# Eighteen small loads ahead of the setup of a decode block, and a clearing of where they land

## The chip, the cores and the metric

The kernel runs on one core of a Trainium2 chip. The metric is the device time of one execution in microseconds (us); it was 242.41 us, the median of two runs (242.36 and 242.45). The engines of the core are PE (TensorE, matmuls), DVE (VectorE), ACT (ScalarE), POOL (GpSimd) and SP (SyncE). Each runs its own list of instructions in order and meets the others only at semaphores. Transfers between the chip's memory (HBM) and the core's on-chip memory (SBUF) are issued by an engine into a DMA queue of its own and are carried by 16 DMA engines. PSUM is the memory that matmuls write.

## The reference

One decode step of a transformer block for four sequences, with modulation by a condition `c`:

```
mod = (silu(c) @ w_mod) -> sa, ca, ga, sb, cb, gb
h   = layernorm(x) * (1 + ca) + sa
q   = h @ wq                                  # 32 heads of 128
p   = softmax(q k^T / sqrt(128))              # 8 KV heads, the last 2048 positions
x   = x + ga * ((p v) @ wo)
h   = layernorm(x) * (1 + cb) + sb
x   = x + gb * ((silu(h @ w1) * (h @ w3)) @ w2)
```

All is float32. What has to be read is about 101 MB: `w_mod`, `wq`, seven KV groups of 8.39 MB each with K and V together, the eighth in two parts, `wo`, `w1`, `w3` and `w2`.

## The kernel before

The weights and the KV cache pass through `ring`, a buffer in SBUF of three slots of 64 KB in each of the 128 partitions. The loads go to the slots in turn: `w_mod_a` (the first third of `w_mod`, with `x` and `c` behind it) to slot 0, `wq` to slot 1, KV group 0 (`kv[0]`) to slot 2, then KV group 1 to slot 0 when `w_mod_a` has been used, KV group 2 to slot 1 when `wq` has been used, group 3 to slot 2 when attention of group 0 is done, and so on to the end. SP issues them all but `wq`, which ACT issues (line 186); each issue waits on SP until its slot is free. A KV group is 128 rows of 64 KB, `w_mod_a` 128 rows of 16.5 KB.

Ahead of the attention stands a setup that needs little data. POOL clears and builds `ident` (the identity for transposes), clears `sc`, `hidT`, `qT` and `xs` (lines 193 to 205), and copies `x` from `w_mod_a` into `xs` (line 273). DVE derives `same`, `avg`, `spread` and `pick` from `ident`. ACT computes `e`, the exponential in silu(c) (line 231). Then come the first layernorm, the modulation out of `w_mod_a` (`mod_a`), `hT`, and with it the issue of KV group 1; then `q` out of `wq`, its transposed form `qT`, the issue of KV group 2, and the groups. A group computes scores on PE into `s_ps`, their maximum on DVE (`nm`), the exponential on ACT into `p_sb`, its transposes, the products with V on PE, and a reduction.

The class `Program` records every operation in the order in which the code is written; the profile gives all of them line 57. For every operand it takes a box: the partitions from the first to the last, and the columns from the lowest to the highest that are touched. An operation waits for an earlier one on another engine, and for an earlier DMA on whatever engine, if their boxes overlap and one of the two writes. A DMA has a semaphore of its own that it raises when it has landed; the wait for it stands in the list of the engine that needs it, ahead of the instruction, so everything behind it on that engine waits too. Before the change, `p_sb`, 128 x 2048, is first written by the exponential of group 0.

Of the kernel before, what the change touches and what calls it, by code (L numbers as in the profile page):

```python
# [11 lines left out]
NT = 4  # L12
# [133 lines left out]
def block_kernel(nc, w_mod_a, wq, kv_in, wo_mod, last_k_wo, last_v, wo, w1, w3, w2, out):  # L146
# [5 lines left out]
    do = Program(nc)  # L152

    def sb(name, *shape):
        return nc.alloc_sbuf_tensor(name, (P, *shape), F32).ap()
# [12 lines left out]
    def bank():  # L168
        turn[0] += 1
        return banks[turn[0] % 2]  # L170

    def load(dst, src, cuts=(0, 1), queue="sync"):
        step = src.shape[1] // cuts[-1]
        for lo, hi in zip(cuts[:-1], cuts[1:]):
            do(queue, "dma_start", dst[:, lo * step : hi * step], src[:, lo * step : hi * step])
        return dst[:, : src.shape[1]]

    def batch(t):

        return t[:, ::8]  # L180
# [6 lines left out]
    do("scalar", "preload_act_table_set", "natural_log_exp_and_others")  # L187
    kv = [None] * G
    kv[0] = load(slots[2], kv_in[0])

# [78 lines left out]


    do("gpsimd", "tensor_copy", batch(xs), xt_sb)
    xp = bank()[:, :P]
    do("tensor", "transpose", xp, xs, ident)
    tot = sb("tot", 1)
# [14 lines left out]
    for half in range(2):  # L291
        qp = s_ps[half]
        for k in range(4):
            for i in range(4):
                at = ((half * 4 + i) * 4 + k) * 512
# [18 lines left out]
            do("tensor", "matmul", a_ps[32 * i : 32 * i + B, :], oT[:, g, i, :], wo_t[g][:, i, :], start=(g == 0), stop=(g == G - 1))  # L314

    mx, nm, ls, l, rl = (sb(n, m) for n, m in (("mx", NT), ("nm", 1), ("ls", NT), ("l", 1), ("rl", 1)))
    p_all = sb("p_sb", NT * 512)
    p_sb = [p_all[:, t * 512 : (t + 1) * 512] for t in range(NT)]
    pT = [sb(f"pT{t}", B, NC, R) for t in range(NT)]
    o_own, o_sum = sb("o_own", NC, P), sb("o_sum", P)  # L320
# [194 lines left out]
```

## Time and profile before

| what | value |
|---|---|
| time, median of two runs | 242.41 us |
| profiled execution, span from the first to the last instruction | 241.1 us |
| the rest of a time, outside the span (242.41 - 241.1) | 1.3 us |
| read from HBM | 101.20 MB, 420 GB/s over the span |
| DMA engines busy | 89.5% by SP's queue, 8.1% by ACT's |
| PE busy | 146.8 us (61%) |
| DVE, ACT, POOL busy | 55.2, 24.0, 2.6 us |

The profile of one execution gives for each instruction its start and length in us from the start of the span, and what ended the idle time before it. A "q" behind an engine's name (SPq, ACTq) is its issuing of DMAs. The DMA rows count packets; q1 is the queue of SP and q10 that of ACT. The packets of q10 are 144: the 128 rows of `wq` and 16 more of nearly no bytes, one on each DMA engine, that close the load and raise its semaphore. The chain of waits follows the work that ended last from its end to the start.

### The profile page before, as it was taken

How to read it: one execution, taken by the hardware profiler on the slowest of the kernel's cores; microseconds unless marked ns; L12 is line 12 of the kernel's file. 1: busy time of each engine (PE TensorE's matmuls, PEld its weight loads, DVE VectorE, ACT ScalarE, POOL GpSimd, SP SyncE). 2: the span in 40 equal slices, each digit the busy share in tenths (PEclk: the TensorE clock that was granted, in tenths of full speed). 3: DMA queues.
4: the chain of work that ended last, by engine and by line, in shares of the span. 5: the costliest groups of instructions: out<-in, count | busy, mean ns of one | idle time of the engine just before them, and what ended most of it. 6: DMA issues, size and time to landing. Idle time of an engine off the chain costs nothing.

```text
span 241.1 us, 2468 instructions
## 1 busy us (share of the span) xinstructions
PE 146.8 (61%) x1103; PEld 52.8 (22%) x1103; DVE 55.2 (23%) x140; ACT 24.0 (10%) x36; POOL 2.6 (1%) x11
## 2 busy tenths in 40 slices
PE   0000169756782972945767586567296919964876
PEld 0000132213222312201311222221131202422333
DVE  4000220240303124123132124130312014103120
ACT  2000000103003003001200300300300000320100
POOL 3000000000000000000000000000000000000000
PEclk9999997995977799779797589797977997996899
DMA  8999989898989898989999999999999999999993
GB/s 316 414 436 425 500 370 500 351 511 359 511 359 503 370 502 370 489 383 478 391 479 391 478 394 468 402 468 405 457 413 424 435 405 435 407 432 426 416 415 133
DMA packets 2889, 101.38 MB, mean 421 GB/s; under 512 B 448, under 2 KB 448, under 8 KB 704
## 3 DMA queue, kind: packets, MB, share of 16 engines
q1 hardware_dynamic: 2736, 92.85, 89.5%
q10 hardware_dynamic: 144, 8.39, 8.1%
q8 instruction: 8, 0.13, 0.2%
q14 instruction: 1, 0.01, 0.0%
HBM read 101.20 MB, written 0.03 MB: 420 GB/s over the span
## 4 chain that ended last, share of the span: by engine, by line
DMA 73%; PE 20%; DVE 3%; ACT 2%; issue 0%; SPq 0%
DMA ring<-kv_in 30%; DMA ring<-wo_mod 17%; DMA ring<-w 15%; DMA ring<-w_mod_a 11%; PE s_ps L57 8%; PE bank L57 7%; PE o_ps L57 4%; PE a_ps L57 2%; ACT p_sb L57 2%; DVE nm L57 2%; DVE p_sb L57 0%; DVE e L57 0%; DVE sq L57 0%; DVE xc L57 0%; DVE tot L57 0%
## 5 line engine op out<-in xcount | busy, mean ns | idle before, releaser
L57 PE MATMUL s_ps<-ring,qT 128*32 128x512 f32 x256 | 37.0, 731 | 20.2 <-DMA ring<-kv_in 14.7
L57 PE MATMUL bank<-ident,p_sb 128*128 128x128 f32 (+1 forms) x136 | 27.4, 350 | 30.8 <-ACT p_sb L57 30.7
L57 PE MATMUL o_ps<-ring,pT 128*16 128x512 f32 x256 | 37.8, 696 | 0.0
L57 PEld LDWEIGHTS bank<-ident,p_sb 128*128 128x128 f32 (+1 forms) x136 | 19.6, 177 | 51.9 <-ACT p_sb L57 31.7
L57 ACT ACTIVATE p_sb<-s_ps,nm 128x2048 f32<-128x2048 f32 (+1 forms) x11 | 16.5, 1501 | 143.2 <-DVE oT L57 105.2
L57 DVE TENSOR_REDUCE nm<-s_ps 128x1 f32<-128x2048 f32 x7 | 16.0, 2292 | 34.5 <-PE s_ps L57 34.5
L57 DVE COPY pT<-bank 128x64 f32<-128x64 f32 x32 | 7.2, 224 | 56.1 <-PE bank L57 56.1
L57 PEld LDWEIGHTS s_ps<-ring,qT 128*32 128x32 f32 x256 | 9.0, 131 | 47.5 <-issue 20.7
L57 PE MATMUL bank<-ident,xs 128*128 128x128 f32 x1 | 0.5, 473 | 27.8 <-POOL xs L57 27.8
L57 PE MATMUL s_ps<-ring,h2T 128*32 128x512 f32 (+1 forms) x64 | 9.1, 664 | 2.3 <-DMA ring<-w 2.3
L57 PE MATMUL a_ps<-ring,oT 128*4 128x512 f32 x64 | 9.1, 709 | 2.0 <-DMA ring<-wo_mod 2.0
L57 PE MATMUL s_ps<-ring,hT 128*32 128x512 f32 x64 | 8.8, 711 | 0.4 <-DVE hT L57 0.4
L57 PEld LDWEIGHTS o_ps<-ring,pT 128*16 128x16 f32 x256 | 5.4, 98 | 11.6 <-issue 9.2
L57 DVE SCALAR_TENSOR_TENSOR o_own<-o_ps,rl,own 128x512 f32<-128x512 f32 x7 | 5.3, 751 | 11.1 <-PE o_ps L57 11.1
L57 DVE TENSOR_REDUCE o_sum<-o_own 128x128 f32<-128x512 f32 x7 | 7.2, 1029 | 0.2
L57 PE MATMUL bank<-ring,sc 128*32 128x256 f32 (+1 forms) x64 | 7.2, 610 | 0.0
L57 PEld LDWEIGHTS bank<-ident,xs 128*128 128x128 f32 x1 | 0.2, 180 | 27.8 <-POOL xs L57 27.8
L57 DVE TENSOR_SCALAR e<-e 128x16 f32<-128x16 f32 x1 | 0.2, 174 | 23.8 <-ACT e L57 23.8
L57 DVE TENSOR_REDUCE mx<-s_ps 128x1 f32<-128x512 f32 x4 | 2.8, 691 | 7.6 <-PE s_ps L57 7.6
L57 DVE COPY qT<-bank 128x64 f32<-128x64 f32 x8 | 2.2, 277 | 9.8 <-PE bank L57 9.4
L57 PEld LDWEIGHTS s_ps<-ring,h2T 128*32 128x32 f32 x64 | 2.6, 129 | 7.4 <-issue 4.5
L57 PE MATMUL s_ps<-ring,hidT 128*32 128x64 f32 (+1 forms) x126 | 3.7, 262 | 0.3 <-DVE hidT L57 0.3
(93 smaller groups left out, 55.4 us busy)
## 6 DMA issues: line engine op xcount, KB each, us to landing
ring<-w SPq DMA_DIRECT2D x2, 3584.0 KB, 38.3
ring<-last_k_wo SPq DMA_DIRECT2D x1, 6144.0 KB, 30.5
ring<-last_v SPq DMA_DIRECT2D x1, 4096.0 KB, 39.9
ring<-w_mod_a SPq DMA_DIRECT2D x1, 2064.0 KB, 26.6
ring<-wo SPq DMA_DIRECT2D x1, 2048.0 KB, 43.4
ring<-w SPq DMA_DIRECT2D x1, 1792.0 KB, 40.9
ring<-w SPq DMA_DIRECT2D x1, 1024.0 KB, 42.9
ring<-w SPq DMA_DIRECT2D x1, 512.0 KB, 43.7
```

What stands on the lines that cost most here:

```text
L57: op = Op(engine, lambda: getattr(getattr(self.nc, engine), method)(*args, **kw), [])
```

## The change

Fifteen loads are put into ACT's list behind `wq` and the table load, and three into POOL's list ahead of its setup. All copy a piece of `w1` that no computation uses into the first 819 columns of `p_sb`, whose allocation moves up for it. After its last piece of setup, POOL clears the first 1024 columns of `p_sb`.

```diff
     do("scalar", "preload_act_table_set", "natural_log_exp_and_others")
     kv = [None] * G
     kv[0] = load(slots[2], kv_in[0])
+    p_all = sb("p_sb", NT * 512)
+    marks = p_all[:, :1024]
+    for n in range(1, 16):
+        do("scalar", "dma_start", marks[:n, 32 * n : 32 * n + 4 * n], w1[:n, 32 * n : 32 * n + 4 * n])
+    for n in range(3):
+        at, m = 512 + 128 * n, 17 + n
+        do("gpsimd", "dma_start", marks[:8, at : at + 64].rearrange("p (s c) -> p s c", s=2)[:, :, :m], w1[:8, at : at + 64].rearrange("p (s c) -> p s c", s=2)[:, :, :m])
...
     do("gpsimd", "tensor_copy", batch(xs), xt_sb)
+    do("gpsimd", "memset", marks, 0.0)
     xp = bank()[:, :P]
...
-    p_all = sb("p_sb", NT * 512)
```

Load n of ACT has n rows of 4n floats and lies at columns 32n to 36n. From n = 9 on its last columns reach into those of load n + 1 (load 9 ends at 324, load 10 begins at 320), and load 15 ends at 540, behind the beginning of POOL's first at 512. The lists show what `Program` makes of that.

ACT's list at the start of the program, before the change (a number in brackets is a semaphore; part0_22_0 is that of `w_mod_a`):

```order
L57 DMA ring<-wq 128x16384 [waits barrier_Pool_Activation_PE_DVE_SP_release]
L57 ACT_TABLE_LOAD
L57 ACTIVATE e<-ring 128x16 [waits part0_22_0]
L57 ACTIVATE ln<-bank,eps_t 128x1 [waits part0_22_tensor,part0_22_vector]
L57 ACTIVATE r<-ln 128x1 [waits part0_22_scalar]
```

And the same place now, from load 7 on; part0_40_12 to part0_40_17 are the semaphores of loads 9 to 14, and part0_40_0 is again that of `w_mod_a`:

```order
L57 DMA p_sb<-w 7x28
L57 DMA p_sb<-w 8x32
L57 DMA p_sb<-w 9x36
L57 DMA p_sb<-w 10x40 [waits part0_40_12]
L57 DMA p_sb<-w 11x44 [waits part0_40_13]
L57 DMA p_sb<-w 12x48 [waits part0_40_14]
L57 DMA p_sb<-w 13x52 [waits part0_40_15]
L57 DMA p_sb<-w 14x56 [waits part0_40_16]
L57 DMA p_sb<-w 15x60 [waits part0_40_17]
L57 ACTIVATE e<-ring 128x16 [waits part0_40_0]
```

Loads 1 to 9 have no wait; each of the loads 10 to 15 stands behind a wait for the landing of the one before it, and `e` now stands behind them all.

POOL's list from the start barrier to its last work, before:

```order
L57 MEMSET ident 128x132 [waits barrier_Pool_Activation_PE_DVE_SP_gather]
L57 ISA [waits part0_22_gpsimd]
L57 AFFINE_SELECT ident<-ident 128x128
L57 MEMSET sc 128x128
L57 MEMSET hidT 128x504
L57 MEMSET qT 128x1024
L57 MEMSET xs 128x128
L57 COPY xs<-ring 128x16 [waits part0_22_0,part0_22_gpsimd]
```

And now; part0_40_18 is the semaphore of ACT's load 15, and those of the last row are of loads that nothing ahead has waited for:

```order
L57 DMA p_sb<-w 8x2x17 [waits barrier_Pool_Activation_PE_DVE_SP_gather,part0_40_18]
L57 DMA p_sb<-w 8x2x18
L57 DMA p_sb<-w 8x2x19
L57 MEMSET ident 128x132
L57 ISA [waits part0_40_gpsimd]
L57 AFFINE_SELECT ident<-ident 128x128
L57 MEMSET sc 128x128
L57 MEMSET hidT 128x504
L57 MEMSET qT 128x1024
L57 MEMSET xs 128x128
L57 COPY xs<-ring 128x16 [waits part0_40_0,part0_40_gpsimd]
L57 MEMSET p_sb 128x1024 [waits part0_40_5,part0_40_6,part0_40_4,part0_40_7,part0_40_21,part0_40_8,part0_40_20,part0_40_9,part0_40_19,part0_40_10,part0_40_11]
```

The wait for load 15 stands at the head of the list, ahead of all of POOL's setup, and the exponential of group 0 on ACT waits for the clearing of `p_sb`. The lists of PE, DVE and SP are the same as before.

## The prediction

> **What bounds the kernel now.** First the page: span, busy share of the DMA engines, and the chain of waits by engine.
>
> ```profile
> span 241.1 us, 2468 instructions
> DMA  8999989898989898989999999999999999999993
> ...
> DMA 73%; PE 20%; DVE 3%; ACT 2%; issue 0%; SPq 0%
> ```
>
> The DMA engines are busy in every slice but the last, and three quarters of the chain is waiting for data. The table of stretches says the same by stage (the last two columns are DMA share and GB/s).
>
> ```profile
> 34.50:47.30 12.80, 10.05 (x72) 3.24 (x73) 2.69 (x11) 1.19 (x2) 0.00 (x0) 0.87 0.95 411
> 47.30:67.30 20.00, 12.34 (x86) 4.58 (x84) 6.34 (x13) 2.06 (x2) 0.00 (x0) 0.83 0.97 419
> 67.30:85.50 18.20, 13.91 (x82) 4.91 (x82) 3.33 (x7) 2.06 (x2) 0.00 (x0) 0.72 1.05 455
> 183.60:229.80 46.20, 33.46 (x239) 11.13 (x239) 9.35 (x32) 5.32 (x14) 0.00 (x0) 0.85 0.98 421
> ```
>
> There is no hole in the stream from which lost time could be won back later. So an edit costs what it holds up the stream of loads, and nothing otherwise. The stream holds as long as the next load is issued before the last one ends. Next, then, the issues of KV groups and the waits for them.
>
> ```profile
> 34.46 0.33 SPq L57 DMA_DIRECT2D ring<-kv_in  x1
> 64.81 59.09 SPq L57 DMA_DIRECT2D ring<-kv_in  x4
> ...
> ring<-kv_in SPq DMA_DIRECT2D x1, 46.9
> ...
> 48.17 1.07 PE L57 MATMUL s_ps<-ring,qT 128*32 128x512 f32 x8 [0.57 <-DMA ring<-kv_in]
> 67.28 5.34 PE L57 MATMUL s_ps<-ring,qT 128*32 128x512 f32 x32 [2.54 <-DMA ring<-kv_in]
> 86.77 3.64 PE L57 MATMUL s_ps<-ring,qT 128*32 128x512 f32 x32 [1.32 <-DMA ring<-kv_in]
> ```
>
> Group 0 is issued at 1.15 (the SP row below) and lands 46.9 us later, at 48.05. Group 1 is issued at 34.46, 13.6 us ahead of that, lands at 67.28, and group 2 at 86.77. In the stream a group takes 19.5 us.
>
> **The change, part by part.** It removes nothing; it adds 18 tiny loads, one clearing and, as the lists show, waits. What decides is when ACT's load 9 lands, since loads 10 to 15, `e`, and all of POOL's setup follow it one by one.
>
> **When load 9 lands.** The issues at the start, and the DMA packets up to 14 us, up to 26 us and from 26 to 27.5 us:
>
> ```profile
> 0.73 0.39 ACTq L57 DMA_DIRECT2D ring<-wq  x1
> 0.74 0.36 SPq L57 DMA_DIRECT2D ring<-w_mod_a  x1
> 1.15 33.64 SPq L57 DMA_DIRECT2D ring<-kv_in  x2
> ...
> q10 hardware_dynamic: 64, 4.19, 70.9%
> q1 hardware_dynamic: 64, 1.06, 20.2%
> ...
> q10 hardware_dynamic: 128, 8.39, 75.4%
> q1 hardware_dynamic: 128, 2.11, 20.3%
> ...
> q1 hardware_dynamic: 32, 1.05, 161.8%
> q10 hardware_dynamic: 16, 0.00, 0.6%
> ```
>
> Two things are read here. Up to 26 us both queues have sent the same number of packets, 64 and 64, then 128 and 128, though a row of `wq` is four times one of `w_mod_a`: a DMA engine takes one packet from one queue, then one from the other. And no row of `kv_in` has gone before `w_mod_a` ends, though it was issued at 1.15: a queue is served in order. In 26 to 27.5 us come the 16 closing packets of `wq`, those of `w_mod_a`, and the first 16 rows of group 0.
>
> So ACT's small loads, issued by about 7 us (9 times the 0.39 us of `wq`'s issue), stay behind `wq` till about 27 us. From then on the two queues take turns again: each small packet goes between two 64 KB rows of group 0, of which each DMA engine has 8 (128 rows by 16). A small load costs an engine that carries it a row and a closing packet; load 9 is the ninth, so the engine that carries all nine has 18 packets to send and 8 turns for them. Even if each load cost but one packet there, nine are more than eight. Load 9 therefore lands with the end of group 0 or just behind, **at 48.3 us** (48.05 and, for what is left of the tiny packets, some 0.3 by my estimate).
>
> The Trainium skill speaks against this: its page "DMA: Bandwidth & Descriptors", section "Queues, rings and completion order", says that an engine takes turns by packets of typically 9 to 17 descriptors. By that, load 9 would be out after one turn; the equal counts above are against it, and its result is the first rival below.
>
> **Loads 10 to 15.** Each waits for the landing of the one before it, now with no other transfer under way. The nearest row is the only small transfer of the trace, the output (KB, us from issue to landing), and how soon ACT starts once its data is there is seen at `e`:
>
> ```profile
> out<-p_sb SPq DMA_DIRECT2D x1, 32.0 KB, 1.5
> ...
> 0.74 26.62 DMA ring<-w_mod_a
> 27.38 0.22 ACT L57 ACTIVATE e<-ring 128x16 f32<-128x16 f32 x1 [24.94 <-DMA ring<-w_mod_a]
> ```
>
> `w_mod_a` lands at 27.36, `e` starts at 27.38. I take 1.6 us for a step, the 1.5 of the output and a little for the wait; six make 9.6, and load 15 lands **at 57.9**. The ends: 1.5 (9.0 in all), since issue and landing can't be shorter than for a transfer that met no other either, and 2.2 (13.2), if reading HBM costs half as much again. The Trainium skill, same page, section "Anatomy of one DMA — SWDGE (gpsimd) path", gives about 2.0 us of fixed cost for a DMA of GpSimd's; six of these would end 2.4 us later than by my value.
>
> **POOL's three loads.** The trace before has no DMA issued by POOL. Bounds per load: the 0.33 us of SP's issue from below, a whole step of 1.6 and as much again for building it from above (3.2). I take 0.9, nearer to the row of an issue, and 2.7 for three, so that `ident` is begun **at 60.6** (ends: 58.9 and 67.5).
>
> **From there to the issue of group 1.** POOL's setup and what DVE makes of it used to lie beside the load of `w_mod_a`, and cost nothing. That cover is gone:
>
> ```profile
> 0.73 0.21 POOL L57 MEMSET ident<- 128x132 f32 x1 [0.29 <-POOLq L508]
> 1.18 0.29 POOL L57 TENSOR_SCALAR_AFFINE_SELECT ident<-ident 128x128 f32<-128x128 f32 x1 [0.23 <-POOL ident L57]
> 2.90 0.20 POOL L57 MEMSET xs<- 128x128 f32 x1
> 27.50 0.21 POOL L57 COPY xs<-ring 128x16 f32<-128x16 f32 x1 [24.39 <-DMA ring<-w_mod_a]
> ...
> 27.76 0.47 PE L57 MATMUL bank<-ident,xs 128*128 128x128 f32 x1 [27.76 <-POOL xs L57]
> ...
> 1.96 0.37 DVE L57 TENSOR_REDUCE same<-ident 128x32 f32<-128x128 f32 x1
> 3.54 0.25 DVE L57 TENSOR_REDUCE pick<-pick_c 128x16 f32<-128x64 f32 x1
> 27.63 0.17 DVE L57 TENSOR_SCALAR e<-e 128x16 f32<-128x16 f32 x1 [23.84 <-ACT e L57]
> 28.27 0.29 DVE L57 COPY x_sb<-bank 128x128 f32<-128x128 f32 x1
> ```
>
> `ident` is begun at 0.73 and ready at 1.47, 0.75 later. DVE's work on it runs from 1.96 to 3.79, 1.83; `e` through DVE from 27.63 to the copy of `x_sb` at 28.27, another 0.64. Together 3.2 us from `ident` to `x_sb`. POOL's own way is no longer: 2.37 us to the end of clearing `xs` (0.73 to 3.10), 0.21 for the copy, 0.5 for PE's transpose (27.76 to 28.27 lies behind the copy), 3.1. From `x_sb` to the issue of group 1 it is 28.27 to 34.46, 6.2. So 9.5 us in all with the steps between engines, and group 1 is issued **at 70.1** instead of 34.46.
>
> **What that does to the stream.** Group 0 has landed at 48.05 and nothing else has been issued: the DMA engines stand still. A load issued into an empty queue takes its 19.5 us and what an issue needs to get going, at most the 1.5 us of the output's whole way; I take 21.2, and group 1 lands at 91.3 instead of 67.28, **24.0 us later**.
>
> Does the delay stay? The issues of groups 2 and 4, and PE's wait for the last K:
>
> ```profile
> 45.73 40.12 SPq L57 DMA_DIRECT2D ring<-kv_in  x3
> ...
> 85.52 39.92 DMA ring<-kv_in
> ...
> 198.26 5.16 PE L57 MATMUL s_ps<-ring,qT 128*32 128x512 f32 x32 [5.45 <-DMA ring<-last_k_wo]
> ```
>
> From group 1's issue, group 2's came 11.3 us later, group 3's 30.4 (64.81). Measured from the new issue, the stream would run dry at 40.7 (two groups, 21.2 + 19.5), so group 3's comes 10 us ahead. Group 0 now ends after group 1 has landed, so attention lags the loads by some 9 us (30.4 less 21.2); but a group's compute is 18.2 us (67.28 to 85.52, when the slot of group 1 was free and group 4 was issued) and its load 19.5, so the lag shrinks by over 1 us in each of the six groups that follow, and the 5.5 us for which PE waited for the last K take the rest. The stream runs on, 24.0 us late, to its end. Clearing `p_sb` (128x1024, as `qT`, whose clearing lies within POOL's 2.37 us above) is done some 4 us after `ident` is begun, 15 us before the exponential of group 0, and costs nothing. Bytes are no matter: 18 loads of less than 4 KB.
>
> The sum is made against the profiled execution: 241.1 + 24.0 = 265.1 us of span, and with the 1.3 us outside it 266.4; I say **266 us**. A difference within 2% of the time, 4.8 us, is about what a measurement of this kernel can tell from no change.
>
> **The rivals.**
> *The small packets don't take turns one by one.* If the first nine loads pass in one turn, load 9 lands at about 29 us, behind one row of group 0 (19.5 / 8 = 2.4 us from 27). Each of loads 10 to 15 then waits for one row (2.4 us, six: load 15 at 44) or for two, one ahead of its data and one ahead of its closing packet (4.9 us, four till 48.6, then two of 1.6: at 52). With 12.2 us to the issue and 21.2 to landing, group 1 lands at 77 to 85, 10 to 18 us late: 252 to 260, middle 257. For it speaks only that no packet as small as these stands among large ones in the trace; against it the equal counts.
> *The handshakes are dear.* Steps at 2.2 and POOL's loads at 2.5 each add 3.6 and 4.8: 275 us. No row excludes it.
> *Not slower.* If the small loads went ahead of the rest of `wq`, load 9 would be there at some 8 us (issues till 7, and the 1.5 of a landing), and six steps of 3.0 (a row of each queue, 19.5 / 8 and a quarter of it) bring load 15 to 26. All is then hidden as long as group 1 is issued by about 46.5, 1.5 ahead of the end of group 0; with 9.5 and 2.7 behind load 15, that is up to a load 15 at 34.3. The price is nothing: 242 us. Against it stands the order within q1, where group 0 stood still behind `w_mod_a` for 25 us.
>
> **How the numbers follow.** My forecast has 0.66, with a range of its own of 262 to 271 (steps from 1.5 to 2.0, POOL's loads from 0.33 to 1.9 each). The first rival has 0.13, the dear handshakes 0.16, not slower 0.04, and 0.01 is for a start that is faster for some other reason. The range reaches into the first rival's upper half and takes in the dear handshakes: **256 to 276**. Slower by over 2% are all but the last two: 0.95; within 2% 0.04; faster 0.01.
>
> **What would show it.** The packets of ACT's queue spread over 27 to 48 us between those of SP's; ACT idle till past 57 us and six issues some 1.6 us apart from 48 us on; `ident` begun at about 60 us; DMA slices near zero from 48 to 71 us and full behind; group 1's issue at 70; the same tail, 24 us later. It is wrong if load 9 lands well before 48, if POOL's loads take more than 2 us each, or if attention of the first groups, started late, becomes the limit behind the hole.

## The result, and the profile after

The changed kernel takes 266.14 us (two runs, 265.97 and 266.31) against 242.41: a ratio of 1.098, 95% interval 1.096 to 1.100. The forecast was 266.0, slower.

The page of the changed kernel: span, the busy tenths of DVE and POOL, the DMA engines' by slices of 6.6 us, and the chain by engine.

```profile
span 264.6 us, 2492 instructions
...
DVE  1000000005205133152241231231332011313031
...
POOL 0000000043000000000000000000000000000000
...
DMA  9999997000897999999899989998999899999994
...
DMA 47%; PE 37%; DVE 7%; ACT 5%; issue 1%; ACTq 1%; POOL 1%; POOLq 0%; DVEq 0%
```

The span is 23.5 us longer than the 241.1 before. Where there was no hole in the DMA row there is now one of three empty slices and parts of the two beside them, and POOL's setup, once in the first slice, lies at its end. The stretch around the hole, with the DMA engines' share and GB/s in its last two columns:

```profile
47.60:69.00 21.40, 4.79 (x37) 2.54 (x37) 5.12 (x26) 0.68 (x3) 5.27 (x11) 1.00 0.13 41
```

The chain of waits in order of time (start, length, what) runs through the hole:

```profile
4.26 43.30 DMA p_sb<-w
47.56 0.02 issue
47.58 1.54 DMA p_sb<-w
...
49.15 1.35 DMA p_sb<-w
...
50.52 1.39 DMA p_sb<-w
...
51.94 1.37 DMA p_sb<-w
...
53.33 1.50 DMA p_sb<-w
...
54.85 1.44 DMA p_sb<-w
56.29 0.29 issue
56.58 1.81 POOL p_sb L57 x3
58.39 0.23 POOL ident L57
```

Load 9, issued at about 4 us, lands at 47.56. Each of the six loads behind it is issued when the one before has landed, and takes 1.35 to 1.54 us; load 15 is there at 56.29. POOL builds its three loads in 1.81 us, and only then begins `ident`. Here are the issue of group 1 on SP, and its time to landing (the view leaves out the KB; the number is us):

```profile
67.70 0.33 SPq L57 DMA_DIRECT2D ring<-kv_in  x1
...
ring<-kv_in SPq DMA_DIRECT2D x1, 23.2
```

Group 1 lands at 90.9 us instead of 67.28, 23.6 us later, and the end comes 23.5 us later.

What kept load 9 for 43 us is read from the packets of the two queues, in stretches of about the time of one 64 KB row (2.42 us). The stretches shown are 28.2 to 30.6, 30.6 to 33.0, 33.0 to 35.4, 37.9 to 40.3, 42.7 to 45.1, and last 45.1 to 47.6.

```profile
q1 hardware_dynamic: 16, 1.05, 100.8%
q10 hardware_dynamic: 9, 0.00, 0.3%
...
q10 hardware_dynamic: 9, 0.00, 0.2%
...
q10 hardware_dynamic: 8, 0.00, 0.2%
...
q10 hardware_dynamic: 7, 0.00, 0.2%
...
q10 hardware_dynamic: 6, 0.00, 0.2%
...
q10 hardware_dynamic: 36, 0.00, 1.0%
q1 hardware_dynamic: 16, 0.00, 0.4%
```

In each stretch but the last SP's queue sends 16 rows, one on each engine (its line is shown once, the others are alike but for the share), and ACT's queue a single small packet on those engines that still have some: first the 9 data rows of the nine engines concerned, then 9 closing packets, then 8 for the eight engines that carry a second load, and so on. The other 36 go together at 45.1 to 47.6, when SP's queue has nothing left but the 16 closing packets of group 0. The nine loads have 90 small packets in all, 45 rows and 45 closings: a load of n rows runs on n engines. That is what the Trainium skill states in "DMA: Bandwidth & Descriptors", section "Why a DMA increments its semaphore by 16 and not by 1". The turns of typically 9 to 17 descriptors that the Trainium skill states on the same page (section "Queues, rings and completion order") are not seen here: a turn is one row or one closing packet.

### The profile page after: what moved, and what is told of

Same layout as the page of the kernel before. It is cut to its first block, busy times and chain, and to the rows that moved or that the text cites. A ratio compares the mean times of both kernels' runs of the same rounds, so it can differ in the third digit from the quotient of the medians.

```text
span 264.6 us, 2492 instructions
## 1 busy us (share of the span) xinstructions
PE 146.2 (55%) x1103; PEld 52.6 (20%) x1103; DVE 55.8 (21%) x140; ACT 24.1 (9%) x36; POOL 5.5 (2%) x15
## 4 chain that ended last, share of the span: by engine, by line
DMA 47%; PE 37%; DVE 7%; ACT 5%; issue 1%; ACTq 1%; POOL 1%; POOLq 0%; DVEq 0%
DMA p_sb<-w 20%; PE s_ps L57 17%; DMA ring<-kv_in 16%; DMA ring<-last_k_wo 12%; PE bank L57 10%; PE o_ps L57 9%; ACT p_sb L57 4%; DVE nm L57 4%; ACTq L57 1%; ACT work L57 1%; PE a_ps L57 1%; POOL p_sb L57 1%; DVE avg L57 0%; DVE sq L57 0%; DVE h L57 0%
## 5 line engine op out<-in xcount | busy, mean ns | idle before, releaser
L57 PE MATMUL bank<-ident,p_sb 128*128 128x128 f32 (+1 forms) x136 | 28.1, 356 | 30.8 <-ACT p_sb L57 30.7
L57 PE MATMUL s_ps<-ring,qT 128*32 128x512 f32 x256 | 35.2, 700 | 11.0 <-DMA ring<-kv_in 5.5
L57 PE MATMUL o_ps<-ring,pT 128*16 128x512 f32 x256 | 38.7, 712 | 0.0
L57 ACT ACTIVATE p_sb<-s_ps,nm 128x2048 f32<-128x2048 f32 (+1 forms) x11 | 16.5, 1501 | 134.7 <-DVE oT L57 94.6
L57 PE MATMUL s_ps<-ring,h2T 128*32 128x512 f32 (+1 forms) x64 | 10.0, 715 | 0.4 <-DVE h2T L57 0.4
L57 DVE COPY oT<-bank 128x16 f32<-128x16 f32 x8 | 1.3, 167 | 12.1 <-PE bank L57 12.1
```

What stands on the lines that cost most here:

```text
L57: op = Op(engine, lambda: getattr(getattr(self.nc, engine), method)(*args, **kw), [])
```

## The experiments

All are variants of the changed kernel, each compared with the kernel before on the same chip.

**Without overlaps between the loads** (e1). POOL's boxes and the cleared columns move along.

```diff
-    marks = p_all[:, :1024]
+    marks = p_all[:, :1152]
     for n in range(1, 16):
-        do("scalar", "dma_start", marks[:n, 32 * n : 32 * n + 4 * n], w1[:n, 32 * n : 32 * n + 4 * n])
+        at = 60 * (n - 1)
+        do("scalar", "dma_start", marks[:n, at : at + 4 * n], w1[:n, at : at + 4 * n])
     for n in range(3):
-        at, m = 512 + 128 * n, 17 + n
+        at, m = 900 + 64 * n, 17 + n
...
```

> All 18 loads and the clearing are kept, but no two loads overlap: ACT's loads lie one behind the other from column 0 to 900, POOL's from 900 on, and POOL clears 1152 columns. So no load waits for another; only the clearing waits for all. Theory (the chain of waits makes a hole in the stream of loads, and the hole is the whole loss): the small loads still go one by one between the rows of group 0 and land at about 47.6 us, but e starts at 27.4 us, group 1 is issued at about 34.5 us and the time is that of before, 242.4 us, within 1 us. First rival (the loads themselves cost, by their packets between the large rows or by POOL building them): most of the 24 us stays, some 260 us or more. Second rival (the clearing of p_sb is late for the exponential of group 0, which starts at 54.3 us in the trace before): the clearing begins at 47.6 us and is done by 49 us, so it too gives 242.4 us here; were the time between, the start of that exponential would show it.

Measured: 257.24 us, ratio 1.062 (1.060 to 1.064; here and below the 95% interval stands in brackets). None of the three forecasts held: 14.8 of some 24 us stay, which is most of them but short of the first rival's 260. The lines are two of POOL's (its loads and the clearing), then the exponential of group 0, the issue of group 3, and the DMA share of the stretch between (last two columns: share, GB/s):

```profile
1.35 1.81 POOL L57 DMA_DIRECT2D p_sb<-w  x3 [0.91 <-POOLq L516]
...
86.31 1.06 POOL L57 MEMSET p_sb<- 128x1152 f32 x1 [58.41 <-DMA p_sb<-w]
...
87.49 1.97 ACT L57 ACTIVATE p_sb<-s_ps,nm 128x2048 f32<-128x2048 f32 x1 [40.35 <-POOL p_sb L57]
...
97.14 0.33 SPq L57 DMA_DIRECT2D ring<-kv_in  x1
...
86.00:98.00 12.00, 8.40 (x60) 3.57 (x64) 1.79 (x7) 2.06 (x2) 1.06 (x1) 0.72 0.00 0
```

The start is undisturbed (`e` at 27.57), so group 1 and group 2 are issued in time (34.72 and 45.98), and just that keeps the small loads waiting: the busiest engine now has 30 small packets, and they find 24 rows to stand behind, those of groups 0 to 2. They are through when the stream runs dry at about 86 us; the clearing, the exponential of group 0 and the issue of group 3 follow, and the hole of 12 us lies there. So the clearing was late for the exponential of group 0, as the second rival has it, but at 86 us; what failed is my figure of 47.6, which took the end of group 0 from the changed kernel, where nothing stands behind it. That the loads cost by themselves is not excluded by this run; e8, below, excludes it.

**Eight loads without overlaps** (e9), and **all eighteen into a tile that is needed late** (e8). e9 is e1 with `range(8, 16)`. e8 has the loads without overlaps in `mod_b` (allocated ahead for it), and clears that:

```diff
-    marks = p_all[:, :1024]
+    mod_b = sb("mod_b", 512)
+    marks = mod_b
     for n in range(1, 16):
+        at = 2 * n * (n - 1)
-        do("scalar", "dma_start", marks[:n, 32 * n : 32 * n + 4 * n], w1[:n, 32 * n : 32 * n + 4 * n])
+        do("scalar", "dma_start", marks[:n, at : at + 4 * n], w1[:n, at : at + 4 * n])
     for n in range(3):
-        at, m = 512 + 128 * n, 17 + n
+        at, m = 128 * n, 17 + n
...
```

with POOL's loads in partitions 64 to 71, where they overlap none of ACT's.

> e1_apart with ACT's loads 8 to 15 alone, into p_sb, POOL's three loads and the clearing kept. Theory: 16 packets on the busiest engine, 16 rows of 2.42 us from 27 us on, so the clearing begins at about 66.5 us and the exponential of group 0 at about 67.7 us, 13.4 us later than in the profile before (54.26). Its end frees the slot for group 3 at about 78 us instead of 64.8, still 7 us ahead of the end of the stream's group 2. So nothing is lost: 242.4 us, up to 243. Rival (a loss in proportion to the loads, eight fifteenths of e1_apart's 14.8 us): 250 us.

> All 18 loads, without overlap as in e1_apart, but into mod_b, a tile that the kernel does not use before about 190 us, and POOL clears mod_b (512 columns) in place of p_sb. Nothing early waits for the loads or for the clearing. Theory, mended after e1_apart (a small load has two packets on an engine, each waits for one 64 KB row of the other queue, and the loads go on waiting as long as the stream is kept full): the engine that carries all fifteen has 30 packets, 30 rows of 2.42 us from 27 us on, so the loads are through and the clearing begins at about 100 us; in e1_apart, where the stream ran dry, it was 86.3 us. Time 242.4 us, within 0.7 us. Rival (the loads cost by themselves, in packets or in POOL's building of them): e1_apart's 257 us or part of it.

Measured: e9 242.95 us, ratio 1.002 (1.001 to 1.003); e8 242.67 us, ratio 1.001 (1.000 to 1.002). The clearings, e9's and e8's, and e9's exponential of group 0:

```profile
64.05 1.06 POOL L57 MEMSET p_sb<- 128x1152 f32 x1 [36.21 <-DMA p_sb<-w]
...
65.22 1.97 ACT L57 ACTIVATE p_sb<-s_ps,nm 128x2048 f32<-128x2048 f32 x1 [18.45 <-POOL p_sb L57]
...
93.20 0.53 POOL L57 MEMSET mod_b<- 128x512 f32 x1 [65.36 <-DMA mod_b<-w]
```

In e8 the loads travel for over 60 us and the time is that of before within 0.2 us: the packets themselves, and POOL's building of its loads, cost next to nothing, and with that e1's first rival is excluded. In e9 the exponential of group 0 is 11 us late and group 3 is issued at 75.3 instead of 64.8, with the stream still full: 0.5 us. Both clearings came earlier than expected, by 2.4 and 6.8 us, one row and three. The closing packets of the groups themselves take turns too (one group had closed by then in e9, three in e8: from 28 to 92 us SP's queue sent 464 packets, 26 rows and three closings on each engine). So 16 small packets meet 15 rows and 30 meet 27: 27 us and 15 or 27 times 2.42 are 63.3 and 92.3, and a little under 1 us to landing.

**Which wait holds the start: POOL's loads behind its setup** (e2), **`e` ahead of loads 10 to 15** (e5), **and both** (e6). e2 moves the three lines of POOL's loads behind `do("gpsimd", "tensor_copy", batch(xs), xt_sb)`; e5 splits ACT's loop:

```diff
-    for n in range(1, 16):
+    for n in range(1, 10):
         do("scalar", "dma_start", marks[:n, 32 * n : 32 * n + 4 * n], w1[:n, 32 * n : 32 * n + 4 * n])
+    e = sb("e", 16)
+    do("scalar", "activation", e, ct_sb, AF.Exp, scale=-1.0)
+    for n in range(10, 16):
+        do("scalar", "dma_start", marks[:n, 32 * n : 32 * n + 4 * n], w1[:n, 32 * n : 32 * n + 4 * n])
...
-    e = sb("e", 16)
-    do("scalar", "activation", e, ct_sb, AF.Exp, scale=-1.0)
```

> POOL's three loads stand behind its setup and the copy into xs, right ahead of the clearing; ACT's list is that of the change. Theory: ident is begun at 0.7 us again, but e still stands behind load 15 and starts at 55.2 us as in the profile of the change. From e to the issue of group 1 it is 7.1 us in the trace before (27.38 to 34.46), so the issue comes at 62.3 us instead of 67.7, and the time is 5.4 us below that of the change: 260.7 us. Rival (POOL's position at the head is the whole cause): the setup is free again, group 1 is issued at about 34.5 us, 242.4 us.

> On ACT, e stands behind load 9 and ahead of loads 10 to 15; POOL's list is that of the change, with its loads at the head. Theory: e runs at 27.4 us, but loads 10 to 15 still wait for load 9 at 47.6 us, load 15 lands at 56.3 us, POOL begins ident at 58.4 us, and DVE needs ident before it comes to e. Group 1 is issued at 67.7 us, the time is that of the change, 266 us, within 1 us. Rival (ACT's late e is the whole cause): group 1 at about 34.5 us and 242.4 us.

> Both: e ahead of loads 10 to 15 on ACT, and POOL's loads behind its setup. Theory: neither e nor ident is late, but the next work of ACT, the logarithm of the first layernorm (ln), stands behind load 15 and starts at about 55.3 us; in the trace before it starts at 30.93 us, 3.5 us ahead of the issue of group 1, so the issue comes at 58.8 us, 8.9 us ahead of the change's, and the time is about 257 us. Rival (the late e and the late ident are the whole cause): 242.4 us.

Measured: e2 260.52 us, ratio 1.075 (1.073 to 1.077), `e` at 55.60 and the issue of group 1 at 62.69; e5 266.23 us, 1.098 (1.096 to 1.100), issue at 68.09. So POOL's place sets the time of the changed kernel, and behind it, 5.6 us shorter, stands ACT's. e6 gave 265.04 us, 1.093 (1.091 to 1.096), where I had said 257. Three lines of its ACT:

```profile
27.45 0.21 ACT L57 ACTIVATE e<-ring 128x16 f32<-128x16 f32 x1 [24.97 <-DMA ring<-w_mod_a]
66.09 7.78 ACTq L57 DMA_DIRECT2D p_sb<-w  x6
73.98 0.26 ACT L57 ACTIVATE ln<-bank,eps_t 128x1 f32<-128x1 f32 x1 [46.32 <-DMA p_sb<-w]
```

The error is that of e1 over again. The issue of group 1 does not hang on `ln`: it needs PE's matmuls with `w_mod_a` (`mod_a`), so it came at 34.6 us, and load 9 stood behind the rows of group 1 too, till 66. `ln` followed at 73.98, `q` and with it the issue of group 2 at 85.98, and the hole opened between groups 1 and 2.

**Fewer loads** (e3: load 15 alone; e4: loads 12 to 15). The only edit is the range of ACT's loop, `range(15, 16)` and `range(12, 16)`.

> Of ACT's loads only load 15 is kept; POOL's three stand at the head of its list and wait for it; the clearing is kept. Theory (small packets take turns with the rows of group 0; only a hole in the stream costs): load 15 has two packets on each engine that carries it and lands after two rows of group 0, at about 33 us. POOL's loads and ident follow as in the profile of the change (2.1 us), ident begins at 35.1 us, and group 1 is issued 9.3 us later, at 44.4 us, 10 us later than before but still about 2 us ahead of the end of group 0's rows. So the time is that of before, 242.4 us, up to 243.5 if the issue comes a little too late. Rival (each us by which group 1 is issued later is lost, since attention starts later): 252 us.

> Of ACT's loads 12 to 15 are kept: load 12 without a wait, and three that wait one for another. Theory: load 12 lands at 33 us after two rows of group 0; each of the next finds rows of group 0 and needs about three of them, so load 13 lands at about 40, load 14 at 45 to 47.5 and load 15, with the stream empty, at 46.6 to 49. Group 1 is issued 11.4 us later, at 58 to 60.3 us, that is 7.4 to 9.7 us ahead of the change's 67.7: 256.4 to 258.7 us. Rival (small packets pass in one turn, and a wait costs 1.45 us each wherever it stands): load 12 at 29, load 15 at 34 us, group 1 issued at 45, and 242 to 243 us.

Measured: e3 242.53 us, ratio 1.001 (1.000 to 1.002); e4 259.17 us, 1.069 (1.067 to 1.071). The chain of e4, then POOL's beginning of `ident` and SP's issue of group 1 in e3:

```profile
1.21 31.09 DMA p_sb<-w
32.32 7.24 DMA p_sb<-w
39.58 7.25 DMA p_sb<-w
46.85 1.54 DMA p_sb<-w
...
34.33 0.23 POOL L57 MEMSET ident<- 128x132 f32 x1
...
43.99 11.49 SPq L57 DMA_DIRECT2D ring<-kv_in  x2
```

The same step costs 7.25 us, three rows, beside the stream, and 1.54 without it. In e3 group 1 is issued 9.5 us later than before and nothing is lost, which the rival (252 us) does not allow: lateness is free until the stream ends. e4 lies 0.5 us above my interval; its group 1 was issued at 60.88, 12.5 us behind load 15, where it is 11.4 in the changed kernel. Of the additional microsecond 0.4 lie in PE's matmuls of `mod_a` (3.64 us against 3.21); there the changed kernel's profile is the odd one, since e1, e3, e5 and e6 have 3.64 too. The other 0.6 lie between PE's transpose of `xs` and the first matmul of the layernorm: DVE's first step on `e` takes 0.98 us instead of 0.16 and runs beside POOL's clearing of `p_sb`, both from 53.24, while in the changed kernel the clearing begins behind that step. That the clearing holds it back was not tested.

**`wq` behind load 15** (e7): the line of `wq`'s load moves behind ACT's loop.

> On ACT, wq is issued behind load 15 instead of ahead of load 1; all else is that of the change. Theory: the small loads now take turns with the 8 short rows that each engine has of w_mod_a and then with the 8 rows of group 0; load 9, with 18 packets on its busiest engine, lands when both are through, at about 28 us, load 15 at 37 us, wq is issued at 36 us, group 1 at 48.4 us. The hole in the stream lies between the end of group 0 (27 us) and the first row of wq (37.4 us, the first row some 0.7 us longer than the others), 10.9 us: about 253 us, and up to 2 more if the later loads, whose issues have little to spare, come late. Rival (load 9 is not bound to the rows of the other queue): load 9 at about 6 us, load 15 at 15 to 20 us, no hole, 242 to 244 us.

Measured: 253.99 us, ratio 1.048 (1.043 to 1.052). Its chain begins

```profile
3.97 23.65 DMA p_sb<-w
27.64 1.33 DMA p_sb<-w
...
35.48 29.05 DMA ring<-wq
```

Load 9 lands at 27.62 and not at 47.56: it is bound to the end of whatever the other queue has, here `w_mod_a` and group 0 alone. The hole lies between 27 us and the first row of `wq`, and costs 11.6 us.

No version is faster than the kernel before; e3, e8 and e9 come to within 0.5 us of it.

## Why the prediction was right

By its own steps, forecast and measured in the profile of the changed kernel:

| step | forecast | measured |
|---|---|---|
| load 9 landed | 48.3 us | 47.56 us |
| loads 10 to 15 | 9.6 us | 8.73 us (47.56 to 56.29) |
| POOL's three loads, with the wait ahead of them | 2.7 us | 2.10 us (0.29 and 1.81) |
| `ident` to the issue of group 1 | 9.5 us | 9.3 us (58.38 to 67.70) |
| issue to landing of group 1 | 21.2 us | 23.2 us |
| group 1 later by | 24.0 us | 23.6 us |
| span | 265.1 us | 264.6 us |

The first step carries the case, and it holds by the packets and by e7 and e8: one small packet, one row. The first rival falls with it: with all nine in one turn, load 9 would have been there at 29 us. "The handshakes are dear" falls by 1.35 to 1.54 us a step and 0.6 us for each of POOL's loads. "Not slower" had its price right and its condition wrong: e3 shows that group 1 issued at 43.99 costs nothing, but the changed kernel's issue comes at 67.70.

The terms that were off partly cancelled. The steps up to the issue of group 1 were 2.4 us too long in all, and its load 2.0 us too short; that the total came within 0.5 us is luck to that extent, though the mechanism doesn't rest on it. I had taken the output's whole way as the most that starting up can cost, and this load took 3.7 us more than the 19.5 of one in the stream. Its packets show where most of that lies. The first row starts 1.0 us after the issue, and the first rows take 2.5 to 3.5 us and not 2.42, so that the last engine comes to its second row 4.4 us after the issue. Seven rows at 2.42 follow. One engine also carries a 16 KB packet of instructions at 79.3 us, and sends its closing packet at 90.41, 1.4 us behind the other 15. What makes the first rows long was not tested. The load behind the hole took 22.7 to 23.2 us in e1, e2, e4 and e5 too.

Some figures of the prediction do not follow from its own rows. 21.2 is 0.2 more than 19.5 and 1.5. The ends named for its own range (steps from 1.5 to 2.0, POOL's loads from 0.33 to 1.9) give 264.1 to 271.8 and not 262 to 271. A step of 1.5 us, which could not be undercut by its argument, was: the six took 1.35 to 1.54, 8.73 in all against its lower end of 9.0. And the clearing of `p_sb` is done 24.5 us ahead of the exponential of group 0 (62.37 and 86.89), where it said 15 and its own issue at 70.1 gives some 25. None of them touches the mechanism.

That the delay stays to the end is as forecast: group 1's lateness, 23.6 us, is that of the end, 23.5. Attention caught up with the loads faster than I said. The scores of groups 1 to 4 start at

```profile
97.31 3.62 PE L57 MATMUL s_ps<-ring,qT 128*32 128x512 f32 x32
114.09 3.62 PE L57 MATMUL s_ps<-ring,qT 128*32 128x512 f32 x32
131.01 3.62 PE L57 MATMUL s_ps<-ring,qT 128*32 128x512 f32 x32
148.97 5.28 PE L57 MATMUL s_ps<-ring,qT 128*32 128x512 f32 x32 [2.36 <-DMA ring<-kv_in]
```

so a group takes 16.8 us and not 18.2, and from group 4 on PE waits for data again, as it did before the change.

What the prediction did not say, and what I learned only from e1 and e6, is that its 48.3 us hold because nothing stands behind group 0. The wait for load 9 and the missing issue of group 1 depend on each other: the loads land because the stream has run dry, and it has run dry because they had not landed.

## What to carry to other kernels

Count the packets that a small load puts on its busiest DMA engine and multiply by the time of the other queue's rows. Beside the 64 KB rows here, each load without a wait took two rows, 4.8 us, and loads that waited for one another three, 7.25 us. Then ask who waits for them, and whether the next large load is issued before the stream ends: until then lateness is nearly free (9.5 us in e3 cost nothing, 10.5 in e9 half a microsecond), and from there on each microsecond is lost (from e4 to the changed kernel the issue of group 1 comes 6.8 us later, and the time is 7.0 us longer). An overlap of a few columns between scratch areas is enough to make such a chain, and a wait at the head of an engine's list holds all that stands behind it.

## What the runs showed that I had not expected

Eighteen loads of some 23 KB in all can be under way for over 60 us: in e8 ACT has issued its last by 7.3 us, and the clearing that waits for them all begins at 93.2, with no loss. In e1, POOL's three, among rows of 64 and 16.5 KB, took 11.0, 16.4 and 21.9 us to land:

```profile
p_sb<-w POOLq DMA_DIRECT2D x1, 1.1 KB, 11.0
...
p_sb<-w POOLq DMA_DIRECT2D x1, 1.1 KB, 16.4
...
p_sb<-w POOLq DMA_DIRECT2D x1, 1.2 KB, 21.9
...
p_sb<-w POOLq DMA_DIRECT2D x1, 1.1 KB, 1.8
```

and 1.8 with the stream empty (the last row, of the changed kernel). A load by ACT takes 1.35 to 1.54 us there from issue to the next issue.

PE, too, showed something: it computes a group's scores in 3.62 us where groups follow one another without a pause, but in 5.28 where it had waited 2.36 us for data. The next group, after 1.96 us, took 5.34, and the one behind it, after 1.19 us, 3.64 again:

```profile
168.43 5.34 PE L57 MATMUL s_ps<-ring,qT 128*32 128x512 f32 x32 [1.96 <-DMA ring<-kv_in]
187.79 3.64 PE L57 MATMUL s_ps<-ring,qT 128*32 128x512 f32 x32 [1.19 <-DMA ring<-kv_in]
```

The profile before has the same pair, 5.34 us after a wait of 2.54 and 3.64 after one of 1.32. The mean granted clock of PE in the two long stretches (148.97 to 154.25 and 168.43 to 173.77) is 0.68, and 1.00 in the short one at 187.79. So a wait of 2.0 to 2.5 us could cost PE 1.7 us beside its own length. But the wait alone doesn't decide it: in e8 the scores at 125.77 took 3.64 us at a clock of 1.00 behind a wait of 2.40. What else decides was not tested.
